# Attention outputs copied out of PSUM before they are scaled, and another plan for the expert blocks, in a top-k attention and mixture-of-experts kernel

## The chip, the cores and the metric

The kernel runs on one core of one Trainium2 chip. A core has five engines with queues of their own, each in order: TensorE (PE in the rows; PEld is its weight load, which overlaps it), VectorE (DVE), ScalarE (ACT), GpSimd (POOL) and SyncE (SP), which here only issues transfers. They wait for each other through semaphores. The metric is the device time of one execution in microseconds; lower is better. Before the change it is 1802.71 us, the median of three runs (1800.99 to 1813.61 us).

## The reference

Eight batches, eight heads, 576 positions of 64 numbers each, all float32. Each query keeps the keys whose score is among its 32 largest. The result, 4608 rows of 512 numbers, goes through a layer of eight experts: each row takes the one expert with the largest logit.

```python
scores = scale * np.matmul(q, k.transpose(0, 1, 3, 2))
kth = np.partition(scores, -32, axis=-1)[..., -32:-32 + 1]
scores = np.where(scores >= kth, scores, -1000000000.0)
attn = softmax(scores)                      # sum + 1e-09 below the line
x = np.matmul(attn, v)                      # to (4608, 512): row, head*64
logits = x @ w_gate                         # (4608, 8)
expert_idx = np.argmax(logits, axis=1)
gate_w = softmax(logits)[row, expert_idx]   # sum + 1e-09 below the line
y[row] = np.maximum(x[row] @ w1[expert], 0) @ w2[expert]   # 512 -> 1024 -> 512
return gate_w[:, None] * y
```

## The kernel before

**Two kinds of work.** The first is attention, in 8 batches of 4 *units*; a unit is a pair of heads of one batch, so there are 32. A unit is worked in 5 *items* (`groups`): four items of two tiles of 128 queries, one for each head, and a fifth of the 64 left-over queries of both. The second is the experts' work, in *blocks* of 128 rows that belong to one expert. A block reads its rows (`xg`), 2 MB of w1 and 2 MB of w2, and writes its rows out.

**One item** goes round the engines: TensorE multiplies q by k into PSUM (`scores`, L213), ScalarE copies the scores to SBUF (`s`, L218), VectorE folds them in two halves (`hl`, L225 and L226) and finds the 32nd largest with MAX8 and MATCH_REPLACE8 (L248 to L269, `thr`), GpSimd makes a bound of it (`low`, L271), ScalarE and GpSimd make the masked scores (`w`, L283 and L293), ScalarE takes the exponential (L296) and sums a row into `z`, TensorE transposes `w` (L309, L317) and ScalarE copies that out (L312, L320). Scores are issued two items ahead of the search.

**One unit** ends in `outputs` (L324): `po` = weights times v (L339), copied to `oT` (L340), transposed back into the PSUM tile `px` (L343) and `pl` (L345), and multiplied by the gate's weights into `pl` (L348). The closure `scaled` that it returns runs later, in `settle`, after the search of the next unit's second item: VectorE takes 1/z (`rz`, L356 to L358), multiplies `px` and `pl` by it on the way into the SBUF rows `x` (L361, L365), does the same for the logits (`lt`, L369) and adds them to `lg` (L373 to L376). `px` and `pl` lie in PSUM until then.

**One batch** ends, in the `settle` of its fourth unit, in `route` (L379): argmax, rank of each row inside its expert, place in the scratch array `x_rows`; five scatters on GpSimd (L420) write the rows there. Then `table` (L442) lists the blocks that are now full: `sure[b]` is the number that must be full after batch b whatever the routing, 0, 2, 6, 11, 15, 20, 24 after batches 0 to 6. After the last batch the table has 19 slots, which with the 24 are the 43 (`NSLOT`) that any routing needs at most; slots without rows read an empty block and are computed like the rest.

**What sets the order.** The loop over 160 items (L605 on) calls `search`, `settle`, `close` (transposes and, at a unit's end, `outputs`), `depths`, `scores` of the item after next, `weights`, and then `pieces`, which issues some of the 17 pieces of a block: its transposes (L506), w1 (L516, rows named `ph`), w2 (L525, `py`). Pieces are issued only from the sixth item of a batch on (`FIRST` = 5), the number being what is left divided by the items left in the batch, so that a batch's blocks are done by its end; in the last batch two blocks (`KEEP`) are held back to cover the last batch's route. A scheduler then sets each engine's order from these calls: it may move an instruction past others of its engine where data allow. Two blocks are loaded ahead (`ahead`, L566), on SP's queue, where the loads of q, k and v stand too (L186, L189); a block's load waits until its rows are scattered. After the last batch `fill_up` writes empty rows behind each expert's last one, and the last table's blocks follow one after another. At the end every engine loads the flag `any_i` (L644) and branches past an exact second version, which does not run.

## Time and profile before

| what | value |
|---|---|
| median of three runs | 1802.71 us (1800.99 to 1813.61) |
| the profiled execution | 1800.4 us; its span, from the first to the last instruction, 1798.7 us |
| busy share of the span | PE 83%, PEld 54%, DVE 71%, ACT 51%, POOL 35% |
| transfers | 244.06 MB, mean 136 GB/s |
| TensorE's granted clock, mean | 0.87 |

The busy shares are means over stages that differ: until about 1453 us attention runs, with blocks between from the third batch on; after that only blocks do, and DVE is idle. So the rows below are read stage by stage. A row of a stretch gives its start and end, its length, then for PE, PEld, DVE, ACT and POOL the busy time in it with the number of instructions, then the granted clock of TensorE (1.00 is 2.4 GHz, 0.50 is 1.2 GHz), the share of the DMA engines and GB/s. A unit is counted from one multiplication of `px` on VectorE (L361) to the next, so the first four of those behind 64.0 us are units 1 to 4. In a row, "busy" is the time in which the engine executes, an idle time is that just before an instruction, and the name behind "<-" is what ended it.

### The profile page before, as it was taken

How to read it: one execution, taken by the hardware profiler on the slowest of the kernel's cores; microseconds unless marked ns; L12 is line 12 of the kernel's file. 1: busy time of each engine (PE TensorE's matmuls, PEld its weight loads, DVE VectorE, ACT ScalarE, POOL GpSimd, SP SyncE). 2: the span in 40 equal slices, each digit the busy share in tenths (PEclk: the TensorE clock that was granted, in tenths of full speed). 3: DMA queues.
4: the chain of work that ended last, by engine and by line, in shares of the span. 5: the costliest groups of instructions: out<-in, count | busy, mean ns of one | idle time of the engine just before them, and what ended most of it. 6: DMA issues, size and time to landing. Idle time of an engine off the chain costs nothing. (4 is left out here: it accounts for less than half of the span.)

```text
span 1798.7 us, 25580 instructions
## 1 busy us (share of the span) xinstructions
PE 1499.2 (83%) x8126; PEld 963.9 (54%) x8126; DVE 1280.0 (71%) x4391; ACT 914.2 (51%) x1845; POOL 624.7 (35%) x876
## 2 busy tenths in 40 slices
PE   5777687679778996999879996999789958999996
PEld 3444444345445663565546654666455536666664
DVE  8999899999999889977788888967799910000000
ACT  5665566657656665655546665655466711111111
POOL 3444444344444434433344344433344420000000
PEclk8667777769967999999959997999788988999999
DMA  1000100061015331644062406433163238888883
GB/s 54 22 21 21 47 28 27 29 233 40 27 47 220 118 141 54 225 167 171 33 238 97 156 34 227 145 131 128 39 234 113 106 101 311 297 303 299 299 297 144
DMA packets 107567, 244.06 MB, mean 136 GB/s; under 512 B 5534, under 2 KB 26014, under 8 KB 107424
## 3 DMA queue, kind: packets, MB, share of 16 engines
q1 hardware_dynamic: 101040, 223.43, 34.7%
q0 software_dynamic: 6384, 18.92, 2.9%
q8 instruction: 66, 1.08, 0.2%
q14 instruction: 77, 0.63, 0.1%
HBM read 221.05 MB, written 23.11 MB: 136 GB/s over the span
## 5 line engine op out<-in xcount | busy, mean ns | idle before, releaser
L293 POOL TENSOR_TENSOR w<-s,w 128x576 f32<-128x576 f32 x288 | 432.2, 1517 | 280.6 <-ACT w L283 278.7
L516 PE MATMUL ph<-xTs,w 128*128 128x128 f32 x2752 | 348.4, 284 | 24.7 <-ACT xTs L508 19.9
L309 PE MATMUL wTm<-ident,w 128*128 128x128 f32 x1152 | 211.0, 325 | 181.0 <-ACT w L296 176.6
L516 PEld LDWEIGHTS ph<-xTs,w 128*128 128x128 f32 x2752 | 328.9, 198 | 53.2 <-ACT xTs L508 27.9
L248 DVE MAX8 tops<-scr 128x8 f32<-128x288 f32 x864 | 355.3, 445 | 1.2
L213 PE MATMUL sc<-qkb 64*128 64x288 f32 (+1 forms) x1280 | 339.9, 522 | 17.5 <-ACT s L218 10.7
L525 PE MATMUL py<-w,hT 128*128 128x512 f32 x688 | 319.5, 610 | 0.0
L296 ACT ACTIVATE w<-w,nbias 128x576 f32<-128x576 f32 x288 | 223.3, 776 | 184.0 <-POOL w L293 182.8
L309 PEld LDWEIGHTS wTm<-ident,w 128*128 128x128 f32 x1152 | 155.3, 165 | 258.0 <-ACT w L296 227.4
L283 ACT ACTIVATE w<-s,low 128x576 f32<-128x576 f32 x288 | 212.7, 774 | 119.9 <-POOL low L271 119.6
L256 DVE MATCH_REPLACE8 scr<-tops,scr 128x288 f32<-128x288 f32 x576 | 250.3, 440 | 0.1
L213 PEld LDWEIGHTS sc<-qkb 64*128 64x128 f32 (+1 forms) x1280 | 164.7, 213 | 112.2 <-issue 41.9
L218 ACT COPY s<-sc 128x576 f32<-128x576 f32 x288 | 175.1, 637 | 59.8 <-PE sc L213 44.2
L525 PEld LDWEIGHTS py<-w,hT 128*128 128x128 f32 x688 | 127.5, 195 | 145.5 <-issue 145.5
L312 ACT COPY wT<-wTm 128x512 f32<-128x512 f32 x256 | 143.9, 586 | 72.0 <-PE wTm L309 71.1
L225 DVE TENSOR_TENSOR hl<-s 128x576 f32<-128x576 f32 (+1 forms) x160 | 131.9, 824 | 56.9 <-ACT s L218 56.0
L530 POOL DMA_INDIRECT out_dram<-y,xg x43 | 43.5, 1012 | 336.0 <-ACT y L529 331.0
L339 PE MATMUL po<-wT,vb 128*64 128x288 f32 x1024 | 151.0, 441 | 8.7 <-ACT wT L314 8.7
L250 POOL TENSOR_SCALAR nbias<-tops 128x2 f32<-128x2 f32 (+1 forms) x160 | 34.9, 218 | 303.9 <-DVE thr L269 178.4
L521 ACT ACTIVATE hT<-ph 128x512 f32<-128x512 f32 x86 | 51.0, 593 | 173.8 <-PE ph L516 173.4
L226 DVE TENSOR_TENSOR hl<-s 128x576 f32<-128x576 f32 (+1 forms) x160 | 127.1, 794 | 0.0
L256 DVE MATCH_REPLACE8 scr<-tops,hl 128x288 f32<-128x288 f32 x288 | 125.4, 440 | 0.0
(115 smaller groups left out, 1283.5 us busy)
## 6 DMA issues: line engine op xcount, KB each, us to landing
w<-in_moe_w_dram SPq DMA_DIRECT2D x86, 2048.0 KB, 12.9
qkb<-in_qk_dram SPq DMA_DIRECT2D x32, 576.0 KB, 3.8
xg<-x_rows SPq DMA_DIRECT2D x43, 257.0 KB, 2.8
vb<-in_v_dram SPq DMA_DIRECT2D x32, 320.0 KB, 3.1
x_rows<-blank SPq DMA_DIRECT2D x9, 257.0 KB, 6.7
out_dram<-y,xg POOLq DMA_INDIRECT x43
x_rows<-x,posi POOLq DMA_INDIRECT x40
wg<-in_moe_w_gate_dram SPq DMA_DIRECT2D x1, 16.0 KB
```

The costliest lines, as they stand in the source:

```text
L213: nc.tensor.matmul(ps[rows, j, 0:HF], n.q[d, cols], n.k[d, j * HF:(j + 1) * HF], start=True, stop=True)
L218: nc.scalar.copy(s[:, m, :, :], ps[:, :, 0:HF])
L248: nc.vector.max(out=tops[:, m, r * 8:(r + 1) * 8], in_=src[m])
L256: nc.vector.match_replace(out=scr[:, m, :], in_to_replace=tops[:, m, r * 8:(r + 1) * 8], in_values=src[m], imm_value=NEG,)
L283: nc.scalar.activation(w[:, m, :], s[:, m, :, :].rearrange("p j k -> p (j k)"), AF.Relu, scale=-STEEP, bias=low[:, m:m + 1],)
L293: nc.gpsimd.tensor_tensor(w[:, m, :], s[:, m, :, :].rearrange("p j k -> p (j k)"), w[:, m, :], op=ALU.subtract)
L296: nc.scalar.activation(w[:, m, :], w[:, m, :], AF.Exp, scale=scale, bias=nbias[:, m:m + 1], accum_out=n.z[:, c + m:c + m + 1],)
L309: nc.tensor.transpose(pm[:, c * P:(c + 1) * P], w[:, m, c * P:(c + 1) * P], ident)
L312: nc.scalar.copy(n.wT[:, :, m, tiles[0] * P:(tiles[0] + 1) * P], pm4)
L339: nc.tensor.matmul(po[r, 0:HF], lhsT, rhs, start=(c == 0), stop=(c == KC - 1))
L516: nc.tensor.matmul(ph[:, f, :], n.w1[:, 0, dt, fc * P:(fc + 1) * P], xT[:, dt, :], start=(dt == 0), stop=(dt == DT - 1),)
L525: nc.tensor.matmul(py, hT[:, f, :], n.w2[:, 0, f, :], start=(f == 0), stop=(f == FT - 1))
```

## The change

`outputs` copies `px`, `pl` and the logits out of PSUM at once on ScalarE, into `x` and `lt`. `scaled` is now a function of its own: 1/z stays on VectorE, and the multiplications by it and the additions to `lg` run on GpSimd, in SBUF. `route` gives back its five scatters as closures, which the loop calls one per item (all at once after the last batch). The blocks listed after batches 0 to 6 are no longer those that must be full but those that usually are (`upto_of`): 0, 4, 8, 13, 17, 22, 26; a slot that is not filled becomes the empty block. They are released (`waiting`, `ahead`) when the batch's scatters have been called, and their pieces are issued at an even `rate` over 20 items, from the sixth item of one batch to the fifth of the next. In the last batch the number is again what is left by the items left. `pinned` ties each of a block's TensorE instructions behind the last attention instruction of TensorE issued before it (`last_pe`, an order without a wait). After the last batch 14 blocks (`ALWAYS`) always run, and the 5 slots that are left of 19 (`spare`) stand behind a branch on the count `rest_i`.

```diff
-    sure = [max(0, -((E * (P - 1) - S * (b + 1)) // P)) for b in range(B - 1)] + [NSLOT]
+    sure = [max(0, -((E * (P - 1) - S * (b + 1)) // P)) for b in range(B - 1)]
+    upto_of = [max(0, (S * (b + 1) - E * ST) // P - 1) for b in range(B - 1)]
+    upto_of = [max(a, c) if b else 0 for b, (a, c) in enumerate(zip(sure, upto_of))]
+    new_of = [b - a for a, b in zip([0] + upto_of, upto_of)]
...
+    LAST = NSLOT - sure[-1]
+    ALWAYS = EB + E // 2 - upto_of[-1]
...
+        nc.scalar.copy(x[:, 0:NC, n.u * P:(n.u + 1) * P], px[:, :].rearrange("p (t d) -> p t d", t=NC))
         pl = bank("pl")
...
+        nc.scalar.copy(x[:, NC, n.u * P:(n.u + 1) * P], pl[:, 0:P])
+        n.lt = k.small.tile([P, KC, 2, E], F32, name="lt")
+        nc.scalar.copy(n.lt, pl[:, P:P + KC * lw].rearrange("p (t h e) -> p t h e", t=KC, h=2))
+
+    def scaled(n, x, lg):
+
+        rz = rz_of[n.u % 2]
+        if not k.exact:
+            nc.vector.tensor_tensor(doubt, doubt, n.over, op=ALU.max)
+        nc.vector.tensor_scalar_add(rz[:, 0:NT], n.z, EPS)
+        nc.vector.reciprocal(rz[:, 0:NT], rz[:, 0:NT])
+        nc.vector.tensor_copy(rz[0:ST, NT:NT + 1], rz[ST:P, NT - 1:NT])
+        rzb = rz[:, :].rearrange("p (t h) -> p t h", h=2)
+        nc.gpsimd.tensor_tensor(n.lt, n.lt, _inner(rzb, E), op=ALU.mult)
+        if n.u:
+            nc.gpsimd.tensor_tensor(lg, lg, n.lt[:, :, 0, :], op=ALU.add)
+            nc.gpsimd.tensor_tensor(lg, lg, n.lt[:, :, 1, :], op=ALU.add)
+        else:
+            nc.gpsimd.tensor_tensor(lg, n.lt[:, :, 0, :], n.lt[:, :, 1, :], op=ALU.add)
+        xu = x[:, :, n.u * P:(n.u + 1) * P].rearrange("p t (h d) -> p t h d", h=2)
+        nc.gpsimd.tensor_tensor(xu, xu, _inner(rzb, D), op=ALU.mult)
...
+    def pinned(put):
+
+        if k.last_pe is not None and not k.exact:
+            tc.add_manual_dep(put.ins, k.last_pe.name, AFTER)
+        return put
+
...
+        def scatter(n):
+            nonlocal left
+            for _ in range(min(n, len(scatters))):
+                scatters.pop(0)()
+            if not scatters and coming:
+                waiting.extend(coming)
+                left += len(coming) * PIECES
+                coming.clear()
                 ahead()
...
+            scatter(1)
             at = i % per_batch
-            if at >= FIRST:
-                rest = left - (KEEP if b == B - 1 else 0)
-                pieces(-(-rest // (per_batch - at)))
+            if at == FIRST and b:
+                rate = new_of[b - 1] * PIECES / per_batch
+            credit += rate
+            room = left - (KEEP if b == B - 1 else 0)
+            if b == B - 1 and at > FIRST:
+                credit = room / (per_batch - at)
+            n_now = min(int(credit + 1e-6), room)
+            credit -= n_now
+            pieces(n_now)
         close(last)
         settle()
-        pieces(left)
+        kept = left - ALWAYS * PIECES
+        assert kept == KEEP
+        pieces(kept)
+        k.last_pe = None
+        pieces(ALWAYS * PIECES)
+        for _ in current:
+            pass
+        more = nc.values_load(rest_i[0:1, 0:1], min_val=0, max_val=LAST)
+        with tc.If(more > ALWAYS):
+            for slot in spare:
+                for _ in block(load_block(*slot)):
+                    pass
```

What this does to the engines' order is shown at three places. The first is VectorE in the `settle` of an ordinary unit in the sixth batch; `rz` is 1/z, `px` and `pl` the PSUM tiles, `hl` the fold of an item. Before:

```order
L356 TENSOR_SCALAR rz_102<-z 128x9
L265 TENSOR_TENSOR both<-tops_94 128x18
L357 RECIPROCAL rz_102<-rz_102 128x9
L269 TENSOR_REDUCE thr<-both 128x2
L358 COPY rz_102<-rz_102 64x1
L361 TENSOR_TENSOR x<-px,rz_102 128x4x128
L365 TENSOR_TENSOR x<-pl,rz_102 128x128
L225 TENSOR_TENSOR hl<-s 128x576
L226 TENSOR_TENSOR hl<-s 128x576
L369 TENSOR_TENSOR lt<-pl,rz_102 128x80
L248 MAX tops_88<-hl 128x8
L373 TENSOR_TENSOR lg<-lg,lt 128x40
```

With the change (its line numbers are higher by some ten):

```order
L373 TENSOR_SCALAR rz_102<-z 128x9
L277 TENSOR_TENSOR both<-tops_94 128x18
L374 RECIPROCAL rz_102<-rz_102 128x9
L281 TENSOR_REDUCE thr<-both 128x2
L375 COPY rz_102<-rz_102 64x1
L237 TENSOR_TENSOR hl<-s 128x576
L238 TENSOR_TENSOR hl<-s 128x576
L260 MAX tops_88<-hl 128x8 x2
L265 MAX tops_88<-hl 128x8 x2
L268 MATCH_REPLACE scr<-tops_88,hl 128x288 x2
```

Between 1/z and the next fold no instruction that reads `px` or `pl` is left, and the logits' instructions are gone from VectorE.

The second is TensorE in the last batch, from the end of its first unit on; `sc` are scores, `wTm` and `wTl` transposed weights, `ph` and `py` a block's two products, `xtp` its transposes. Before:

```order
L348 MATMUL pl<-wg_72,oT_96 128x16 x5
L213 MATMUL sc<-qkb 128x288
L516 MATMUL ph<-xTs,w_11835 128x128 x12
L213 MATMUL sc<-qkb 64x288
L309 MATMUL wTm<-ident,w 128x128 x8
L213 MATMUL sc<-qkb 64x288 x3
L516 MATMUL ph<-xTs,w_11835 128x128 x2
L317 MATMUL wTl<-ident,w 64x128 x2
L516 MATMUL ph<-xTs,w_11835 128x128
L309 MATMUL wTm<-ident,w 128x128 x4
L516 MATMUL ph<-xTs,w_11835 128x128 x3
L309 MATMUL wTm<-ident,w 128x128 x4
```

With the change:

```order
L522 MATMUL xtp<-ident,xg 128x128 x4
L321 MATMUL wTm<-ident,w 128x128 x7
L532 MATMUL ph<-xTs,w_11288 128x128 x32
L541 MATMUL py<-w_11290,hT 128x512 x8
L522 MATMUL xtp<-ident,xg 128x128 x4
L321 MATMUL wTm<-ident,w 128x128
L329 MATMUL wTl<-ident,w 64x128 x2
L225 MATMUL sc<-qkb 128x288
L532 MATMUL ph<-xTs,w_12319 128x128 x32
L541 MATMUL py<-w_12321,hT 128x512 x8
L522 MATMUL xtp<-ident,xg 128x128 x4
L225 MATMUL sc<-qkb 128x288 x2
```

Where a block's pieces stood between transposes and scores, three whole blocks (32 `ph` and 8 `py` each; the third's `py` follow the last row) now stand one behind another with three of the four score products of one item between them. In batches 3 to 7 the pieces stay spread: each unit's rows hold the pieces of one block, or of one and a quarter where the list has five.

The third is GpSimd around the scatters of the third batch; `x_rows` is the scratch array. Before:

```order
L271 TENSOR_SCALAR low<-thr 128x2
L274 TENSOR_TENSOR over<-tops_90,thr 128x2
L293 TENSOR_TENSOR w<-s,w 128x576 x2
L250 TENSOR_SCALAR nbias<-tops_92 128x2
L420 DMA x_rows<-x,posi 38016x514 x5
L271 TENSOR_SCALAR low<-thr 128x2
L274 TENSOR_TENSOR over<-tops_92,thr 128x2
L250 TENSOR_SCALAR nbias<-tops_94 128x2
```

With the change:

```order
L283 TENSOR_SCALAR low<-thr 128x2
L286 TENSOR_TENSOR over<-tops_90,thr 128x2
L384 TENSOR_TENSOR x<-x,rz_102 128x5x128
L377 TENSOR_TENSOR lt<-lt,rz_102 128x80
L379 TENSOR_TENSOR lg<-lg,lt 128x40
L380 TENSOR_TENSOR lg<-lg,lt 128x40
L305 TENSOR_TENSOR w<-s,w 128x576 x2
L262 TENSOR_SCALAR nbias<-tops_92 128x2
L427 DMA x_rows<-x,posi 38016x514 x5
L283 TENSOR_SCALAR low<-thr 128x2
L286 TENSOR_TENSOR over<-tops_92,thr 128x2
```

The multiplication and the logits' instructions are new, and the five scatters still stand together, as they do in every batch from the third on; only in the first two are they apart.

## Rows read from the trace of the kernel before

**Rows 1.** The page: busy us, share of the span and instructions by engine.

```profile
PE 1499.2 (83%) x8126; PEld 963.9 (54%) x8126; DVE 1280.0 (71%) x4391; ACT 914.2 (51%) x1845; POOL 624.7 (35%) x876
```

**Rows 2.** Busy by stretch: batches, end; us, PE PEld DVE ACT POOL, clock, DMA.

```profile
64.00:397.30 333.30, 239.65 (x1144) 138.50 (x1142) 319.11 (x1078) 204.04 (x418) 145.99 (x202) 0.72 0.16 56
397.30:567.10 169.80, 139.08 (x739) 86.83 (x738) 160.95 (x550) 104.87 (x215) 74.02 (x104) 0.82 0.24 85
567.10:744.40 177.30, 152.97 (x917) 97.89 (x916) 159.12 (x550) 111.20 (x228) 74.87 (x106) 0.96 0.38 137
744.40:944.60 200.20, 175.78 (x943) 114.48 (x944) 158.10 (x550) 110.51 (x222) 78.08 (x106) 0.86 0.39 142
944.60:1128.10 183.50, 160.03 (x916) 101.50 (x918) 160.19 (x550) 112.04 (x228) 76.01 (x107) 0.92 0.37 130
1128.10:1333.80 205.70, 181.16 (x996) 115.30 (x992) 159.24 (x550) 114.99 (x234) 80.54 (x107) 0.88 0.39 139
1333.80:1453.40 119.60, 109.93 (x643) 70.47 (x641) 100.46 (x332) 75.62 (x156) 47.66 (x69) 0.94 0.26 93
1453.40:1798.70 345.30, 297.48 (x1684) 214.76 (x1682) 7.45 (x44) 46.99 (x80) 24.37 (x25) 0.96 0.73 266
```

**Rows 3.** The same of single units: without blocks, with route, with blocks.

```profile
103.50:144.10 40.60, 28.68 (x144) 16.47 (x142) 39.62 (x129) 25.41 (x54) 17.60 (x24) 0.71 0.08 23
184.60:231.00 46.40, 32.59 (x146) 19.20 (x144) 41.29 (x148) 25.70 (x54) 20.65 (x30) 0.71 0.12 41
993.20:1036.70 43.50, 42.11 (x245) 26.25 (x244) 38.15 (x129) 27.79 (x58) 16.69 (x26) 1.00 0.40 136
```

**Rows 4.** Groups by line: busy us, mean ns, idle before and its releaser.

```profile
L312 ACT COPY wT<-wTm 128x512 f32<-128x512 f32 x256 | 143.9, 586 | 72.0 <-PE wTm L309 71.1
...
L361 DVE TENSOR_TENSOR x<-px,rz 128x512 f32<-128x512 f32 x32 | 22.1, 692 | 79.7 <-PE px L343 79.6
...
L374 DVE TENSOR_TENSOR lg<-lg,lt 128x40 f32<-128x40 f32 x24 | 11.5, 481 | 0.2
...
L373 DVE TENSOR_TENSOR lg<-lg,lt 128x40 f32<-128x40 f32 x24 | 10.1, 420 | 0.2
L365 DVE TENSOR_TENSOR x<-pl,rz 128x128 f32<-128x128 f32 x32 | 9.2, 289 | 11.5 <-PE pl L348 11.5
...
L322 ACT COPY wTt<-wTl 64x128 f32<-64x128 f32 x32 | 8.3, 259 | 0.0
L369 DVE TENSOR_TENSOR lt<-pl,rz 128x80 f32<-128x80 f32 x32 | 7.4, 230 | 0.0
```

**Rows 5.** One line each: ns min/median/max, first and last start.

```profile
L374 DVE TENSOR_TENSOR lg<-lg,lt x24: 176/199/1075, 106.6 to 1455.3; 128x40 f32<-128x40 f32 x24
...
L225 DVE TENSOR_TENSOR hl<-s x160: 434/749/1930, 9.4 to 1432.1; 128x576 f32<-128x576 f32 x128, 128x288 f32<-128x288 f32 x32
...
L293 POOL TENSOR_TENSOR w<-s,w x288: 1392/1410/2717, 20.4 to 1441.6; 128x576 f32<-128x576 f32 x144
```

**Rows 6.** The order of time, TensorE, one block of the last stage: start, us.

```profile
1506.28 0.60 PE L506 MATMUL xtp<-ident,xg 128*128 128x128 f32 x4
...
1507.74 7.41 PE L516 MATMUL ph<-xTs,w 128*128 128x128 f32 x64 [0.86 <-ACT xTs L508]
...
1514.99 7.03 PE L525 MATMUL py<-w,hT 128*128 128x512 f32 x16
...
1521.86 0.60 PE L506 MATMUL xtp<-ident,xg 128*128 128x128 f32 x4
```

**Rows 7.** The page, transfers: KB each, median us from issue to landing.

```profile
w<-in_moe_w_dram SPq DMA_DIRECT2D x86, 2048.0 KB, 12.9
```

**Rows 8.** The branch at the end, in the queues: ns min/median/max, starts.

```profile
L644 POOLq TENSOR_LOAD <-any_i x1: 496/496/496, 1787.8 to 1787.8; - x1
...
L645 PEldq COMPARE_BRANCH  x1: 3355/3355/3355, 1781.4 to 1781.4; - x1
...
L645 POOLq INC_SWDGE_SEM x1: 1859/1859/1859, 1789.1 to 1789.1; - x1
```

More of the change, by code (lines that the diff above doesn't have):

```diff
@@ L14 @@
 AX = mybir.AxisListType
+AFTER = mybir.DependencyInfo(mybir.DependencyClass.NoSync, mybir.DependencyReason.DATA)
 WAIT = mybir.DependencyInfo(mybir.DependencyClass.Sync, mybir.DependencyReason.DATA)
@@ L152 @@
     nc.vector.tensor_copy(run, e_at)
+    rest_i = const.tile([1, 1], I32, name="rest_i")
     done = const.tile([1, E], F32, name="done")
@@ L322, in transposed, with outputs @@
             nc.scalar.copy(n.wTt[:, :, SM:S], pt[0:ST, 0:P].rearrange("p (h q) -> p h q", h=2))
-    def outputs(n):
-        rz = rz_of[k.unit % 2]
+    def outputs(n, x):
         oT = oT_of[k.unit % 2]
@@ L417, in route, with scatter @@
         mine = []
-        for i in range(KC):
+        def scatter(i):
             r = slice(0, P if i < NC else ST)
@@ L427, in route @@
                 mine.append(put)
-        scattered.extend(mine)
+                scattered.append(put)
+        return [lambda i=i: scatter(i) for i in range(KC)]
     def fill_up():
@@ L472, in table @@
         )
[L473 to L477 removed]
+        none = sm.tile([1, NSLOT], F32, name="none")
+        nc.vector.tensor_scalar(none[:, 0:n], slots[:, 0:n], upto[:, E - 1:E], float(EMPTY), ALU.is_ge, ALU.mult)
+        nc.vector.tensor_tensor(slot_f[:, 1, 0:n], slot_f[:, 1, 0:n], none[:, 0:n], op=ALU.max)
+        nc.vector.tensor_scalar_min(slot_f[:, 1, 0:n], slot_f[:, 1, 0:n], float(EMPTY))
         slot_i = sm.tile([1, 2, NSLOT], I32, name="slot_i")
         nc.vector.tensor_copy(slot_i[:, :, 0:n], slot_f[:, :, 0:n])
[L480 removed]
+        if last:
+            nc.vector.tensor_copy(rest_i, upto[:, E - 1:E])
+        else:
             nc.vector.tensor_tensor(upto, left, upto, op=ALU.subtract)
@@ L546 @@
         x_of, lg_of = {}, {}
-        waiting = []
-        loaded = []
+        waiting, loaded, coming, spare, scatters = [], [], [], [], []
         current = None
@@ L574, in close @@
             if g == groups[-1]:
-                late = (b, u, outputs(n))
+                if u == 0:
+                    x_of[b] = k.xp.tile([P, KC, XW], F32, name="x")
+                    token_ids(x_of[b][:, :, Dm + 1].bitcast(I32), b)
+                    lg_of[b] = k.small.tile([P, KC, E], F32, name="lg")
+                outputs(n, x_of[b])
+                late = (b, u)
                 b2, u2 = divmod(b * U + u + 2, U)
@@ L583, in settle @@
                 return
-            b, u, scaled = late
+            b, u = late
             late = None
-            if u == 0:
-                x_of[b] = k.xp.tile([P, KC, XW], F32, name="x")
-                token_ids(x_of[b][:, :, Dm + 1].bitcast(I32), b)
-                lg_of[b] = k.small.tile([P, KC, E], F32, name="lg")
-            scaled(x_of[b], lg_of[b])
+            scaled(unit_of[b, u], x_of[b], lg_of[b])
             if u < U - 1:
                 return
-            route(x_of[b], lg_of[b])
+            scatters.extend(route(x_of[b], lg_of[b]))
             if b == B - 1:
+                scatter(KC)
                 fill_up()
-            new = sure[b] - (sure[b - 1] if b else 0)
+            new = LAST if b == B - 1 else new_of[b]
             if new:
                 slot_i = table(new, b == B - 1)
-                waiting.extend((slot_i[0:1, 0, j:j + 1], slot_i[0:1, 1, j:j + 1]) for j in range(new))
-                left += new * PIECES
+                coming.extend((slot_i[0:1, 0, j:j + 1], slot_i[0:1, 1, j:j + 1]) for j in range(new))
+                if b == B - 1:
+                    spare.extend(coming[ALWAYS:])
+                    del coming[ALWAYS:]
+            if b == B - 1:
+                scatter(0)
+        def scatter(n):
[6 more added lines that the diff above has]
+                coming.clear()
                 ahead()
@@ L611 @@
         last = None
+        credit = rate = 0.0
         for i, (b, u, g) in enumerate(work):
@@ L666 @@
                         transposed(n, g, w)
-                    outputs(n)(x, lg)
-                route(x, lg)
+                    outputs(n, x)
+                    scaled(n, x, lg)
+                for put in route(x, lg):
+                    put()
                 nc.vector.tensor_scalar_add(ids, ids, S)
```

51 lines of the change are left out of this document (11 added, 40 removed).

## The prediction

> **What bounds the kernel now.** The busy shares of the page name no engine: TensorE has 83% of the span, VectorE 71% [rows 1]. The busy times by stretch do. Up to 397 us there are no blocks: a unit takes 40.60 us and VectorE is busy for 39.62 of them [rows 3], so VectorE bounds it. From the third batch on there are blocks, and a batch takes 169.8, 177.3, 200.2, 183.5 and 205.7 us while VectorE stays at 158 to 161 [rows 2]: it waits there for 9 to 46 us a batch. In a unit of that stage TensorE is busy for 42.11 of 43.50 us at the full granted clock [rows 3]. After 1453 us there are only blocks, each 15.6 us after the one before: 0.60 + 7.41 + 7.03 us of TensorE and 0.86 us of waiting for ScalarE [rows 6].
>
> The groups by line say what VectorE waits for: its multiplication of `px` stood idle for 79.7 us in 32 units and that of `pl` for 11.5 us, both until TensorE was done [rows 4]. So whenever TensorE has blocks in front of a unit's last products, VectorE, which is in order, stops there, and the search of the next items is late too.
>
> **The change, part by part.**
>
> *Scaling on GpSimd.* Five kinds of instruction leave VectorE: 22.1 + 9.2 + 7.4 + 10.1 + 11.5 us [rows 4], with those of a batch's first unit 62.5 us, or 1.95 us a unit. With them go the two waits. The copies cost ScalarE 0.59 us for `px` (the copy of 128x512) and about 0.26 us each for `pl` and `lt` (that of 64x128 has the same 128 elements a partition) [rows 4]: 1.1 us a unit on an engine that is busy for 27.8 of 43.5 us [rows 3], so nothing. If that cover were gone it would be 1.1 us a unit, 35 us in all. On GpSimd the multiplication of `x` has 640 elements a partition where the nearest row, `w`, has 576 and takes 1.41 us, 2.72 at most [rows 5]: 1.6 us, at most 3.0. With the logits I take 2.3 us a unit, and GpSimd is busy for 17 of 41 us [rows 3]: hidden as well.
>
> What isn't hidden is that the two engines get into each other's way. An addition to `lg` on VectorE takes 199 ns at the median and 1075 at most, a fold 749 and 1930 [rows 5]: the long ones are those that meet a multiplication on GpSimd. A fold that is met loses up to 1.2 us. Bounds for the new work: no fold met, 0; two a unit, 2.4 us. I take 0.6, one fold in two units, since the new multiplication begins after the copies and so mostly behind the two folds that follow 1/z. So a unit bound by VectorE loses 1.95 us of work and 0.9 us of waiting and gets 0.6 back: 2.2 us less.
>
> The Trainium skill speaks against this part (SBUF — State Buffer, "Who interferes with whom"): GpSimd and a VectorE instruction with two SBUF inputs take one shared read interface, and the later one is blocked for the whole of the earlier. The long rows of L374 and L225 agree with it.
>
> *A unit with route.* It takes 46.40 us without blocks [rows 3]. VectorE's first step of `route` needs `lg`, which now comes by ScalarE (1.1 us) and GpSimd (2.3 us), where VectorE itself took 2 us. So only about 1 us is won in such a unit. The scatters are five in a row again from the third batch on (the order above), so spreading them gives nothing there.
>
> *Blocks over 20 items instead of 15.* TensorE's work for attention in a unit: the unit with 42.11 us held 36 `ph`, 13 `py` and 4 transposes of blocks, which by [rows 6] are 36/32 x 7.41 + 13/8 x 7.03 + 0.60 = 20.4 us; 21.7 us are left. With one block a unit (lists of four) TensorE needs 21.7 + 15.0 = 36.7 us, VectorE 38.15 - 1.95 + 0.6 = 36.8. With one and a quarter (lists of five) TensorE needs 21.7 + 18.8 = 40.5 us. A unit can't be shorter than that; where one engine clearly bounds it, it was 1.4 us longer [rows 3]. Two engines that are even cost each other more: I take 41 us for the first (between 37 and the row's 43.5) and 43.5 for the second (between 40.5 and, with the 6 us that separate 37 from 43.5, 46.5). Units with route: 45.5 and 47, and 45 in the seventh batch's, which holds few pieces.
>
> *The pieces of the last batch.* The number to issue is computed with `room` = left - KEEP, which is negative while fewer than 34 pieces are left, in the first five items. Then `n_now` is negative and `credit` grows, so that the sixth item issues all it has at once. The order shows it: three blocks in a row in the second unit. They take 3 x 15.6 = 47 us of TensorE. Of the next items only one is scored ahead and not yet searched, 8 us of VectorE (40.60 / 5, [rows 3]). So VectorE stands still for 39 us, and nothing makes it up. This stretch was 119.6 us with 100.46 us of VectorE [rows 2]; now it is 100.5 - 3 x 1.95 + the same 19 us of idle time + 39 = 153 us.
>
> *Fewer blocks.* By the reference's own inputs the experts get 620, 519, 615, 513, 642, 507, 554 and 638 rows, which is 40 blocks; in the lists after batches 0 to 6 no slot stays empty, and 14 are left for the end: the branch isn't taken. Where 24 + 19 blocks ran, 26 + 14 do. The end has 16 blocks (2 kept) instead of 21. The two kept ones now run whole behind the last unit, 31 us, and the gap that they cover is longer (from 1453.4 us to 15.6 us before 1506.3, 37 us [rows 2, 6]): hidden. So 5 x 15.6 = 78 us go.
>
> *The branch.* Each engine loads a register and jumps; on GpSimd, which ends last, 0.50 + 1.86 us [rows 8]; TensorE's compare stood for 3.36 us, though under its own matmuls. Bounds 2.4 and 5.8; I take 3. The last unit's scaling goes by ScalarE and GpSimd, 2 us later than before: the gap is that much longer.
>
> The Trainium skill (Runtime: NRT & Kernel Launch, "Instruction fetch mechanics") says that a taken branch to a target outside the fetched window has to wait for a fetch; no row here shows one by itself. The bounds above don't use it.
>
> *The sum*, against the profiled execution [rows 2]: before 64.0 us nothing. To 397.3 us: 6 x 2.2 + 2 x 1 = 15 less. The five batches with blocks: 169.8 to 168.5, 177.3 to 168.5, 200.2 to 177.5, 183.5 to 168.5, 205.7 to 175.5: 78 less. The last batch: 33 more. The end: 78 less, 2 + 3 more. 1798.7 - 15 - 78 + 33 - 73 = 1665.7 us, with the 1.7 us that lie around the span 1667.4. The median of the three runs is 2.3 us above the profiled one, which is no more than their spread; I say 1668 us.
>
> **Rivals.**
>
> *GpSimd takes over VectorE's wait.* Its `lt` and `x` wait for the same `px` and stand in order before the next `w`; if that holds the scores' buffers, units with blocks stay as they were. For it: GpSimd waits in the same place in its order. Against it: VectorE still has two scored items in hand, 16 us. Then the 78 us are not won: 1746 us.
>
> *The lock.* If two folds a unit are met (2.4 us), the 20 units that VectorE bounds or nearly so (8 + 9 + 3) lose 1.8 us more: 1704 us; with GpSimd's multiplication at 3.0 us and the other units hit too, 1668 + 31 x 1.8 = 1724 us. The rule of the Trainium skill named above (SBUF — State Buffer, "Who interferes with whom") would make it this one.
>
> *The units come down to their floor*, 37 and 40.5 us: 9 x 4 + 6 x 3 = 54 us less, 1614; half of that, 1641 us, is likelier.
>
> *The change doesn't skip what it says.* If more than 14 blocks were left, the five spare ones run: 78 us more, and a pipeline that starts anew, some 15: 1761 us. The row counts speak against it.
>
> *Slower than before: the weights.* Pinned pieces stand in TensorE's order in front of attention; if a block's weights come late, everything stops. A load takes 12.9 us [rows 7]; uncovered in all 24 blocks, 310 us: 1978 us. From 134 / 24 = 5.6 us a block it is slower than before. Against it: SP issues a block's load when the block two before is done, and a block now lasts 33 to 41 us.
>
> **The numbers.** The forecast as worked out, 0.64; GpSimd takes over the wait 0.10; the lock 0.12; the floor 0.09; spare blocks run 0.01; weights late 0.04, of which half is slower than before and half within a percent of it. The low end, 1628, is halfway into the floor; the high end, 1725, is the lock at its worst; outside lie the rivals beyond and the rest of the floor, about 0.2. A measurement of this kernel can tell about 1%, 18 us: faster 0.96, the same 0.02, slower 0.02.
>
> **What would show it.** Right: VectorE's idle time in front of a read of `px` gone, with no like wait in front of its folds; units of 41 us where a list has four, 43 to 44 where it has five; in the last batch one hole of about 39 us in VectorE while TensorE does 96 `ph` and 24 `py`; 16 blocks at 15.6 us behind the last unit; the branch under 6 us. Wrong: folds that wait for `s` as long as they waited for `px`; folds at 1.9 us at the median; long waits of `ph` for a transfer; the hole absent; or a block cadence other than 15.6 us.

## The result

The median is 1705.33 us (four runs, 1699.89 to 1713.96) against 1802.59 us for the kernel before: a ratio of 0.945 (0.940 to 0.951). The change makes the kernel 97 us faster; 135 were forecast. The profiled execution took 1705.1 us, its span 1703.2.

The busy time by stretch, with borders that answer to those of [rows 2]: a stretch runs from the transposed `px` of a batch's first unit to that of the next batch's first unit, the last batch's to that of its last unit (columns as there, with the number of instructions in brackets):

```profile
63.80:398.60 334.80, 256.31 (x1137) 145.89 (x1135) 308.07 (x1054) 210.87 (x444) 163.59 (x234) 0.68 0.15 50
398.60:572.80 174.20, 159.88 (x901) 100.64 (x899) 153.31 (x516) 115.98 (x237) 84.53 (x118) 0.94 0.38 134
572.80:745.60 172.80, 161.99 (x903) 101.74 (x901) 156.14 (x534) 115.52 (x237) 85.37 (x121) 0.94 0.39 139
745.60:922.70 177.10, 163.90 (x972) 103.22 (x972) 153.92 (x539) 114.64 (x239) 83.40 (x124) 1.00 0.46 158
922.70:1100.50 177.80, 164.68 (x918) 103.95 (x916) 156.53 (x528) 117.09 (x240) 87.22 (x119) 0.94 0.39 138
1100.50:1277.80 177.30, 155.07 (x888) 97.08 (x888) 157.32 (x543) 112.50 (x235) 79.96 (x119) 0.93 0.35 123
1277.80:1434.30 156.50, 126.86 (x654) 78.44 (x652) 98.10 (x316) 80.96 (x167) 53.95 (x81) 0.79 0.36 129
1434.30:1703.20 268.90, 238.86 (x1361) 172.71 (x1359) 5.96 (x40) 39.13 (x68) 22.60 (x25) 0.97 0.72 258
```

Beside the forecast:

| stretch | before | forecast | after | after less forecast |
|---|---|---|---|---|
| to the second batch's end | 333.3 | 318.3 | 334.8 | +16.5 |
| third batch | 169.8 | 168.5 | 174.2 | +5.7 |
| fourth | 177.3 | 168.5 | 172.8 | +4.3 |
| fifth | 200.2 | 177.5 | 177.1 | -0.4 |
| sixth | 183.5 | 168.5 | 177.8 | +9.3 |
| seventh | 205.7 | 175.5 | 177.3 | +1.8 |
| last batch | 119.6 | 153 | 156.5 | +3.5 |
| the end | 345.3 | 272.3 | 268.9 | -3.4 |

At the ends of the batches the borders of [rows 2] lie where VectorE begins to wait for `px`, 0.5 to 4.9 us before its multiplication starts. By the starts of the multiplications the stretches before are 333.9, 170.2, 176.8, 204.6, 181.7, 203.3, 118.9 and 345.3 us; the sum of the forecast is the same by both.

So four of the eight stretches are within 4 us, and the miss of 37 us sits where a unit has no block or one block. A unit without blocks was 40.60 us and is 40.60 us, though VectorE is busy 2 us less in it than in [rows 3]; one with route is not shorter either:

```profile
127.50:168.10 40.60, 32.46 (x141) 17.96 (x141) 37.60 (x124) 26.31 (x56) 18.79 (x28) 0.67 0.08 23
168.10:214.60 46.50, 32.11 (x144) 18.77 (x144) 42.30 (x143) 26.42 (x56) 24.16 (x34) 0.72 0.13 46
```

In the unit without blocks VectorE stands idle for 3.0 us now, where it was 1.0 us in [rows 3]. What it waits for (us in total, times, longest us), before, beside the 79.6 us in front of its read of `px` [rows 4], and now:

```profile
DVE hl L225 <- ACT s L218: 56.0, 32, 5.5
```

```profile
DVE hl L237 <- ACT s L230: 150.3, 51, 40.9
DVE mx L388 <- POOL lg L380: 23.4, 8, 13.4
```

The wait for `px` is gone, and the fold of the copied scores waits instead: 150.3 us, of which 40.9 are the hole in the last batch. Of the 23.4 us in front of `mx`, the first step of `route`, 13.4 lie behind the last unit, 3.8 and 4.1 in the first two batches, and at most 0.5 in each of the others.

**Where ScalarE stands.** The same place in a unit without blocks, ScalarE in order of time (start, us; in brackets the idle time before and what ended it). Before:

```profile
102.91 1.18 ACT L218 COPY s<-sc 128x576 f32<-128x576 f32 x2
103.97 1.46 ACT L283 ACTIVATE w<-s,low 128x576 f32<-128x576 f32 x2
106.28 0.78 ACT L296 ACTIVATE w<-w,nbias 128x576 f32<-128x576 f32 x1 [0.86 <-POOL w L293]
...
107.54 1.07 ACT L312 COPY wT<-wTm 128x512 f32<-128x512 f32 x2 [0.39 <-PE wTm L309]
```

After:

```profile
103.62 1.18 ACT L230 COPY s<-sc 128x576 f32<-128x576 f32 x2
104.69 0.61 ACT L355 COPY x<-px 128x512 f32<-128x512 f32 x1
...
106.92 1.07 ACT L324 COPY wT<-wTm 128x512 f32<-128x512 f32 x2 [1.30 <-PE wTm L321]
107.88 0.79 ACT L295 ACTIVATE w<-s,low 128x576 f32<-128x576 f32 x1
...
111.10 0.78 ACT L308 ACTIVATE w<-w,nbias 128x576 f32<-128x576 f32 x1 [1.05 <-POOL w L305]
```

And two rows of VectorE after, the end of that item's search and the fold that then stands:

```profile
102.86 0.15 DVE L281 TENSOR_REDUCE thr<-both 128x2 f32<-128x18 f32 x1
```

```profile
122.10 0.76 DVE L237 TENSOR_TENSOR hl<-s 128x576 f32<-128x576 f32 x1 [2.94 <-ACT s L230]
```

The search ends at 103.0 us, and the depths (`w<-s,low`), the next step of that item, start 4.9 us later. Ahead of them in ScalarE's order stand the three new copies (one row of three is shown) and two copies of transposed weights, for which ScalarE waits 1.30 us more. Before, the depths started at 103.97 us, and the copies of transposed weights stood behind them. So the order changed by more than the three copies: in the 31 units behind the first, the second item's depths stood ahead of the first item's copies of transposed weights in all 31 before, and do so in 11 now. The exponential, which follows by way of GpSimd, comes at 111.10 where it came at 106.28; the copies of the scores of a later item stand behind that; and the fold waits 2.94 us for them.

### The profile page after: what moved, and what is told of

The parts are those of the page before. It is cut to its first block, busy times and chain, and to the rows that moved or that the text cites. A ratio compares the mean times of both kernels' runs of the same rounds, so it can differ in the third digit from the quotient of the medians.

```text
span 1703.2 us, 24993 instructions
## 1 busy us (share of the span) xinstructions
PE 1470.7 (86%) x7874; PEld 927.9 (54%) x7874; DVE 1245.2 (73%) x4258; ACT 940.7 (55%) x1929; POOL 683.8 (40%) x993
## 5 line engine op out<-in xcount | busy, mean ns | idle before, releaser
L305 POOL TENSOR_TENSOR w<-s,w 128x576 f32<-128x576 f32 x288 | 427.9, 1498 | 263.9 <-ACT w L295 263.3
L225 PE MATMUL sc<-qkb 64*128 64x288 f32 (+1 forms) x1280 | 358.7, 514 | 7.7 <-DMA qkb<-in_qk_dram 5.6
L321 PE MATMUL wTm<-ident,w 128*128 128x128 f32 x1152 | 219.5, 330 | 158.0 <-ACT w L308 157.0
L532 PE MATMUL ph<-xTs,w 128*128 128x128 f32 x2560 | 325.9, 286 | 16.3 <-ACT xTs L524 12.9
L532 PEld LDWEIGHTS ph<-xTs,w 128*128 128x128 f32 x2560 | 308.2, 199 | 44.6 <-issue 20.9
L321 PEld LDWEIGHTS wTm<-ident,w 128*128 128x128 f32 x1152 | 156.5, 167 | 256.5 <-ACT w L308 235.3
L541 PE MATMUL py<-w,hT 128*128 128x512 f32 x640 | 294.6, 601 | 0.0
L237 DVE TENSOR_TENSOR hl<-s 128x576 f32<-128x576 f32 (+1 forms) x160 | 141.3, 883 | 150.6 <-ACT s L230 150.3
L541 PEld LDWEIGHTS py<-w,hT 128*128 128x128 f32 x640 | 115.5, 191 | 122.5 <-issue 122.2
L238 DVE TENSOR_TENSOR hl<-s 128x576 f32<-128x576 f32 (+1 forms) x160 | 131.7, 823 | 0.0
L260 DVE MAX8 tops<-hl 128x8 f32<-128x288 f32 x288 | 125.4, 441 | 0.0
```

Source lines behind the costliest of these rows:

```text
L225: k.last_pe = nc.tensor.matmul(ps[rows, j, 0:HF], n.q[d, cols], n.k[d, j * HF:(j + 1) * HF], start=True, stop=True).ins
L260: nc.vector.max(out=tops[:, m, r * 8:(r + 1) * 8], in_=src[m])
L305: nc.gpsimd.tensor_tensor(w[:, m, :], s[:, m, :, :].rearrange("p j k -> p (j k)"), w[:, m, :], op=ALU.subtract)
L321: nc.tensor.transpose(pm[:, c * P:(c + 1) * P], w[:, m, c * P:(c + 1) * P], ident)
L532: pinned(nc.tensor.matmul(ph[:, f, :], n.w1[:, 0, dt, fc * P:(fc + 1) * P], xT[:, dt, :], start=(dt == 0), stop=(dt == DT - 1),))
L541: pinned(nc.tensor.matmul(py, hT[:, f, :], n.w2[:, 0, f, :], start=(f == 0), stop=(f == FT - 1)))
```

## The experiments

Each ratio is against the kernel before, in the same set of runs. Medians of the kernel before in these sets: 1804.85, 1804.70 and 1802.37 us.

**The scaling back on VectorE, the rest of the change kept.**

```diff
-        nc.scalar.copy(x[:, 0:NC, n.u * P:(n.u + 1) * P], px[:, :].rearrange("p (t d) -> p t d", t=NC))
...
-        nc.gpsimd.tensor_tensor(xu, xu, _inner(rzb, D), op=ALU.mult)
+        nc.vector.tensor_tensor(xu[:, 0:NC], px[:, :].rearrange("p (t h d) -> p t h d", t=NC, h=2),
+            _inner(rzb[:, 0:NC, :], D), op=ALU.mult)
```

> The changed kernel with the scaling as it was before: VectorE multiplies px and pl out of PSUM in settle; the block plan, the pins and the branch stay. Theory Q (the scaling's move won nothing, since ScalarE's three copies and GpSimd's multiplications stand in front of an item's w and the next s and made the fold wait instead): units without blocks stay at 40.5 us, the whole within 15 us of 1705, 1695 to 1720. Rival U (the move took VectorE out of TensorE's queue and made the units with blocks short): the wait for px is back, 60 to 90 us in all, and the whole is 1735 to 1765 us. Rival L (the two engines meet at SBUF): folds fall from 883 to 824 ns at the mean, 14 us, and the whole is about 1690.

Measured: 1699.0 us, 0.942 (0.938 to 0.946). The intervals of this kernel and of the whole change overlap: the change without its first part is as fast as with it. That is theory Q. The units with blocks stay short although VectorE waits for `px` again; the fifth batch takes 178.0 us, where the whole change has 177.1 and the kernel before 204.6:

```profile
DVE hl L237 <- ACT s L230: 81.4, 24, 41.8
DVE x L376 <- PE px L354: 38.3, 19, 8.9
```

```profile
738.70:916.70 178.00, 165.99 (x960) 104.31 (x959) 158.27 (x551) 112.67 (x227) 74.93 (x109) 0.98 0.44 154
```

So it isn't the freed `px` that shortened the batches with blocks. And in a unit without blocks (41.0 us) no fold waits.

**The kernel before with the scaling moved, and nothing else.** The edit is the first part of the diff alone (copies on ScalarE, products on GpSimd).

> The kernel before with the scaling's move alone: copies on ScalarE, multiplications on GpSimd; the block plan is that of before. Q: 1790 to 1815 us, the same as before, with VectorE's wait for px (91 us) gone and its wait for s up from 56 by 80 to 110 us. U: 1740 to 1770. L: slower by some 14 us, 1815, with longer folds.

Measured: 1805.45 us, 1.001 (0.998 to 1.003): no change. Its waits:

```profile
DVE hl L225 <- ACT s L218: 153.2, 51, 8.6
DVE mx L376 <- POOL lg L368: 35.4, 8, 12.6
```

The 79.6 + 11.5 us in front of `px` and `pl` are gone, the folds' wait has grown from 56.0 to 153.2 us, and `mx` adds 35.4. So 133 us of waiting came for 91 that went, and the difference is about what VectorE's busy time fell by (from 1280.0 to 1241.2 us). The fifth batch stays long:

```profile
757.60:959.80 202.20, 180.29 (x983) 116.65 (x982) 155.53 (x548) 116.77 (x240) 87.67 (x122) 0.87 0.40 142
```

**The pieces of the last batch issued evenly.**

```diff
-            n_now = min(int(credit + 1e-6), room)
-            credit -= n_now
+            n_now = max(0, min(int(credit + 1e-6), room))
+            credit = min(credit - n_now, 1.0)
```

> The changed kernel with the number of pieces kept from going negative and the credit capped at one: the last batch's three blocks are spread over its last 15 items. If the three blocks in a row cost what the prediction says (a hole of about 39 us in VectorE, 33 us more than before in the last batch): 1665 to 1675 us, and the hole is gone. If the blocks only move the same wait to later units: 1690 to 1705.

Measured: 1677.15 us, 0.930 (0.926 to 0.933), 28 us less than with the bunch. The end of the changed kernel's bunch: the last of its three blocks on TensorE with the scores behind it, and then the fold on VectorE that waited for them:

```profile
1312.54 7.41 PE L532 MATMUL ph<-xTs,w 128*128 128x128 f32 x64 [0.18 <-ACT xTs L524]
1319.79 7.03 PE L541 MATMUL py<-w,hT 128*128 128x512 f32 x16
1326.75 0.75 PE L225 MATMUL sc<-qkb 64*128 64x288 f32 x2
```

```profile
1328.20 0.76 DVE L237 TENSOR_TENSOR hl<-s 128x576 f32<-128x576 f32 x1 [40.88 <-ACT s L230]
```

With even pieces the longest wait in front of a fold is 5.8 us, and the last batch takes 117.4 us instead of 156.5. TensorE's granted clock in that batch is 0.99 where it was 0.79: with the bunch no block was left behind it to stand between the attention's products, and from 1370 us on the clock was 0.64. So the 28 us are the hole and this together.

**GpSimd's multiplication of x made small.** It scales one column in 64 only, so most of `x` stays unscaled; the instruction stays in its place.

```diff
-        nc.gpsimd.tensor_tensor(xu, xu, _inner(rzb, D), op=ALU.mult)
+        nc.gpsimd.tensor_tensor(xu[:, :, :, 0:1], xu[:, :, :, 0:1], _inner(rzb, 1), op=ALU.mult)
```

> The changed kernel with GpSimd's multiplication of x by 1/z cut to one of 64 columns (the rest of x is left unscaled; the routing doesn't use it): an instruction of 640 elements becomes one of 10, and some 1.1 us a unit leave GpSimd. If GpSimd's part of Q is the loop's cost: 25 to 35 us less, 1670 to 1680. If ScalarE's copies are: 1698 to 1707. L: folds shorter, 14 us less, 1690.

Measured: 1713.49 us, 0.950 (0.945 to 0.954), not faster than the whole change (0.940 to 0.951). The multiplication fell from 1259 to 231 ns, and the folds' wait stayed:

```profile
L384 POOL TENSOR_TENSOR x<-x,rz 128x10 f32<-128x10 f32 x32 | 7.4, 231 | 28.0 <-ACT x L364 28.0
...
L237 DVE TENSOR_TENSOR hl<-s 128x576 f32<-128x576 f32 (+1 forms) x160 | 133.3, 833 | 146.9 <-ACT s L230 146.7
```

Neither the time of that multiplication nor its meeting VectorE is what holds the units. GpSimd still stands for 28.0 us in front of it until ScalarE's copies are done; this run leaves that as it was.

**The depths first on ScalarE.** The changed kernel; `depths` is called before `settle` and `close`, and the copies of transposed weights are ordered behind it.

```diff
+            w = depths(g, s_of[i], low)
             settle()
             if last is not None:
                 close(last)
-            w = depths(g, s_of[i], low)
...
+    def behind(copy):
+        if k.last_act is not None and not k.exact:
+            tc.add_manual_dep(copy.ins, k.last_act.name, AFTER)
```

> The changed kernel with one thing moved: an item's depths (the Relu on ScalarE that follows the search) are put ahead of the previous unit's copies out of px and pl, and the copies of the transposed weights are held behind them. Theory S (it is the place of the new copies in ScalarE's order that eats what VectorE saves: in a unit without blocks the depths start 3.9 us later than before, the scores' copy with them, and the fold stands for 2.9 us): a unit without blocks takes 37.5 to 39 us where it took 40.4, and the whole 1665 to 1690 us. Theory G (the work on GpSimd, or the engines' shared reading, holds the unit, whatever ScalarE's order): 40 to 41 us a unit and 1698 to 1712 us. Held copies can also cost: if the transposed weights come late for the outputs, units with blocks get longer and the whole is above 1712.

Measured: 1639.35 us, 0.909 (0.906 to 0.912): 66 us less than the whole change, below the range of theory S. A unit without blocks takes 36.3 us, all of it VectorE's:

```profile
85.20:121.50 36.30, 27.42 (x142) 15.56 (x142) 36.24 (x124) 26.02 (x55) 18.67 (x28) 0.78 0.08 26
```

ScalarE in order of time, where the search had ended at 99.1 us:

```profile
99.54 0.78 ACT L296 ACTIVATE w<-s,low 128x576 f32<-128x576 f32 x1 [1.45 <-POOL low L284]
...
101.55 0.59 ACT L361 COPY x<-px 128x512 f32<-128x512 f32 x1 [0.28 <-PE px L360]
...
102.96 0.79 ACT L309 ACTIVATE w<-w,nbias 128x576 f32<-128x576 f32 x1
```

The depths now wait for `low`, which is to say that ScalarE is there before its input is; the copies run while GpSimd makes `w`. The copies are as long as they were. Only their place differs. GpSimd stands in front of its multiplication of `x` for 24.1 us here too (29.1 in the changed kernel), so that wait isn't what held the units either.

Of the 4.3 us between 40.60 and 36.30, VectorE's idle time makes 2.9 (from 3.0 to 0.1) and its busy time 1.4 (from 37.60 to 36.24).

**The depths first, the copies of transposed weights not held.** The first half of that edit alone.

> The changed kernel with the depths issued before the previous unit's copies, but without holding the copies of the transposed weights behind them: those go where they went, ahead of the depths in many items. Theory S1 (the three copies out of px and pl, 1.1 us, are what delays the depths): as with all held, 1639 us, at most 1650. Theory S2 (it is the copies of transposed weights and TensorE's transposes that they wait for, and the new copies only came on top): the units without blocks stay at 39.5 to 40.5 us, the whole 1680 to 1705 us.

Measured: 1715.58 us, 0.950 (0.945 to 0.954), not separable from the change by itself, and outside the ranges of both theories. A unit without blocks, and ScalarE at the place shown above:

```profile
126.50:166.00 39.50, 31.73 (x141) 17.95 (x142) 36.48 (x124) 26.17 (x56) 18.91 (x29) 0.67 0.08 24
```

```profile
104.59 0.61 ACT L355 COPY x<-px 128x512 f32<-128x512 f32 x1
...
107.64 1.45 ACT L295 ACTIVATE w<-s,low 128x576 f32<-128x576 f32 x2
```

The depths still stand behind the three new copies, 5.7 us after the search ended (101.9 us). The second item's depths are ahead of the copy of `px` in 7 of the 31 units behind the first; in the changed kernel it is 6, and in the run before this one all 31. So the earlier call alone doesn't put the depths first, since the scheduler orders ScalarE anew; only with the hold do they come first. VectorE's idle time in the unit is 3.0 us, as with the change by itself, and the 1.1 us that it is shorter are one instruction's: the maximum into `doubt`, 128x9 elements, takes 0.14 us here and 1.25 us there, where it meets a multiplication of GpSimd.

So this run doesn't tell S1 from S2. Without the three copies (the run with the scaling back) no fold waits in such a unit, so they bring the wait; whether by their own 1.1 us or by the copies of transposed weights that come to stand in front as well was not told apart. The granted clock doesn't decide it: this unit has 0.67 and the one before it 0.72, and both take 39.50 us.

**The kernel before with the depths first.** Both halves of the edit, without any of the change.

> The kernel before with the depths first and the copies of the transposed weights held behind them, all else as it was. Theory C (before the change ScalarE's order cost little, since VectorE was busy for 39.62 of 40.60 us in a unit without blocks, and stood for px where there are blocks): at most 1 us a unit without blocks, the whole 1785 to 1808 us. Rival D (the order held the units with blocks before the change too, the waits for px being a consequence of it): 1720 to 1775 us.

Measured: 1767.02 us, 0.981 (0.977 to 0.986): 35 us less, outside theory C's range and inside rival D's. The order on ScalarE cost the kernel before as well. VectorE's idle time in front of `px` is down from 79.6 to 63.8 us:

```profile
DVE x L368 <- PE px L350: 63.8, 17, 9.2
```

and in a unit without blocks VectorE's busy time, with the same instructions as in [rows 3], from 39.62 to 37.6 us:

```profile
86.50:126.90 40.40, 29.95 (x142) 16.60 (x142) 37.62 (x129) 25.53 (x52) 16.50 (x24) 0.71 0.08 23
```

**Fewer blocks at the end, in the kernel before.**

```diff
-                waiting.extend((slot_i[0:1, 0, j:j + 1], slot_i[0:1, 1, j:j + 1]) for j in range(new))
+                run_new = new if b < B - 1 else new - 3
+                waiting.extend((slot_i[0:1, 0, j:j + 1], slot_i[0:1, 1, j:j + 1]) for j in range(run_new))
```

> The kernel before, with the last list's three slots that are empty at the end not run, so that 24 + 16 blocks run instead of 24 + 19. Nothing else is changed. Theory B (a block behind the last unit is worth its cadence of 15.6 us): 3 x 15.6 = 47 us less, about 1756 us. Rival: the end is also bound by the loads of weights or the stores, and a block fewer is worth less, 1765 to 1790 us.

Measured: 1757.28 us, 0.972 (0.968 to 0.977): 47 us for three blocks (42 to 58 by the interval), 15.8 each.

**Even pieces without the pins**, the run with even pieces where `pinned` ties nothing.

> The changed kernel with even pieces in the last batch and without the pins that hold a piece in its place in TensorE's order. Theory P0 (the order on TensorE is the same with and without pins, but for the last batch and the first list): within 6 us of the run with even pieces alone, 1671 to 1683 us. Rival P1 (pins win by holding a block's pieces apart): 1690 us or more. Rival P2 (pins lose, since TensorE stands in order behind a piece): 1665 us or less.

Measured: 1677.09 us, 0.928 (0.925 to 0.931), the same as with the pins. They neither win nor lose here.

**Three combinations.** Even pieces with the scaling back on VectorE:

> The changed kernel with two parts changed: the scaling stands on VectorE again, straight out of PSUM, and the last batch's pieces are issued evenly (the number to issue is never negative and credit is not saved up). If the two act apart, as the run with the scaling back (6 us less) and the run with even pieces (28 us less) have them: 1671 us. If the even pieces need the freed px (VectorE waits again for px in the last batch): 1680 to 1700 us. If GpSimd's copies were the cost of the route units in the last batch as well: 1660 to 1668 us.

Measured: 1654.36 us, 0.917 (0.914 to 0.919). That is 23 us less than even pieces alone, and less than each of the three expectations: without the depths first, the move of the scaling costs time once the bunch is gone. The two edits did not act apart. In the profiled executions the difference lies in the third and the sixth batch above all: 165.5 and 170.2 us here, 177.7 and 179.8 with even pieces alone.

Depths first and even pieces:

> The changed kernel with the depths first, as in the run of that, and with even pieces in the last batch. If the two act apart (1639 for the first, 28 us less for the second): 1611 us. If VectorE, which waits less for the scores with the depths first, loses as much to the bunch as with the scaling back (46 us): 1593 us. If TensorE bounds the last batch anyway: 1625 us or more.

Measured: 1602.15 us, 0.888 (0.885 to 0.891), the fastest of all: 103 us below the change as it stands and 200 below the kernel before. Even pieces give 37 us here, between the 28 and the 46 of the expectation.

The same with the scaling back on VectorE:

> The changed kernel with depths first, even pieces, and the scaling back on VectorE out of PSUM. Theory M (with ScalarE's order mended, the move of the scaling to GpSimd is worth what VectorE saves, some 2 us in a unit bound by VectorE): units without blocks 38 to 39.5 us, 15 to 40 us more than depths first with even pieces. Rival N (the move is worth nothing in any order, since GpSimd and ScalarE give it back in units with route and blocks): within 10 us of it, and below 1620 us.

Measured: 1605.55 us, 0.891 (0.887 to 0.894), not separable from the run before it, as rival N has it for the whole. But they get there by different ways. The units without blocks are longer with the scaling on VectorE, as theory M has it:

```profile
88.10:128.50 40.40, 29.94 (x142) 16.56 (x144) 37.60 (x131) 25.52 (x52) 16.53 (x24) 0.71 0.08 23
128.50:166.70 38.20, 28.10 (x142) 15.79 (x144) 37.59 (x130) 25.35 (x52) 16.51 (x24) 0.77 0.08 25
```

VectorE is busy for 37.6 us in both, 1.0 us more than in such a unit with the scaling on GpSimd (36.64 of 36.70 us). The 2.2 us between the two rows are TensorE's: in the first, 16 products of `po` take 4.11 us at a granted clock of 0.50, in the second 2.16 us at 1.00, and VectorE waits 2.3 us for `px` in the first alone. To the second batch's end the run with the scaling on VectorE takes 322.1 us and the other 308.1. It wins 5.0 of these 14 us back in the six batches that follow, and 4.5 at the end (267.0 against 271.5 us).

## Why the prediction came out as it did

**Right: the fewer blocks.** Five blocks at 15.6 us were the largest safe term. The end took 268.9 us where 272.3 were forecast, the cadence is that of [rows 6], and the run with three blocks fewer gave 47 us by itself:

```profile
1501.58 0.60 PE L522 MATMUL xtp<-ident,xg 128*128 128x128 f32 x4
...
1517.16 0.60 PE L522 MATMUL xtp<-ident,xg 128*128 128x128 f32 x4
```

**Right: the branch.** The last `py` ended 11.8 us before the end of the span before the change (1786.9 of 1798.7) and ends 14.3 us before it now: 2.5 us, 3 forecast. The last `py`, before and after:

```profile
1779.90 7.03 PE L525 MATMUL py<-w,hT 128*128 128x512 f32 x16
```

```profile
1681.85 7.03 PE L541 MATMUL py<-w,hT 128*128 128x512 f32 x16
```

**Right: the bunch in the last batch.** Forecast a hole of 39 us and a last batch 33 us longer; measured a hole of 40.88 us and 36.9 us longer, and 28 us of the whole when it is undone.

**Right in size, wrong in reason: batches with longer lists.** The fifth and seventh came out at 177.1 and 177.3 us (177.5 and 175.5 forecast). The prediction gave VectorE's freedom from `px` as part of the reason. But with the scaling back on VectorE the batches are as short (178.0 and 182.5 us), and with the scaling moved alone they stay long (202.2 and 199.0), so as far as that reason goes the size came out by luck. The pins are ruled out by the run without them. What is left of the change there is that the 17 pieces of a block are spread over 20 items instead of 15, and, in the seventh batch, that one block less lies in it (62 rows of `py` against 80, 16 to a block). This is concluded from what is left; the spreading was not run by itself.

**Wrong: the stretch without blocks (16.5 of the 37 us, of which 6 x 2.2 = 13 were the units without route).** The step that failed is "1.1 us a unit on an engine that is busy for 27.8 of 43.5 us [rows 3], so nothing". VectorE's part of the sum held: 1.95 - 0.6 = 1.35 us less of busy time was forecast, and it went from 39.62 to 37.60, 2.0 less. But its idle time went from 1.0 to 3.0 us, 2.9 of them in front of one fold, where the sum had it fall by 0.9. ScalarE's busy share was taken for cover. ScalarE is in order and stands in the loop by which one item's search leads to the scores of a later one (search, `low`, depths, `w`, exponential, copy of the scores, fold). Its idle time is spent waiting inside that loop, so a copy ahead of the depths pushes the loop, whatever the share. The run with the depths first shows it: same copies, same GpSimd work, 36.3 us a unit, of which VectorE is idle for 0.1. The prediction had priced the lost cover at "1.1 us a unit, 35 us in all"; that this is near the miss of 37 us is luck, since such a unit loses 2.9 us and the batches with longer lists lose nothing.

**Wrong by the same step: units with route and lists of four (19.3 of the 37 us, in the third, fourth and sixth batches).** The miss lies in the three units with route: they take 51.1, 52.2 and 52.1 us where 45.5 was forecast, 18.9 of the 19.3 us; the nine units between them take 41.0 on the mean, and 41 was forecast. The unit with route of the fourth batch with the change, with the scaling back on VectorE, and with the depths first:

```profile
693.40:745.60 52.20, 45.70 (x246) 30.54 (x244) 43.84 (x162) 30.36 (x63) 26.49 (x35) 0.87 0.46 164
```

```profile
690.70:738.70 48.00, 42.19 (x246) 27.30 (x244) 45.62 (x178) 28.30 (x57) 22.59 (x32) 0.93 0.54 192
```

```profile
657.60:703.60 46.00, 40.99 (x236) 25.39 (x234) 42.96 (x164) 30.16 (x62) 24.39 (x36) 0.93 0.56 198
```

The prediction looked at `lg`, which comes later ("only about 1 us is won in such a unit"). That wait cost 0.5 us here, and some 4 us only in the first two batches. Of the 8.4 us for which VectorE is idle in the first row, 5.3 lie in front of folds. With the depths first the three units take 142.0 us instead of 155.4: that is 13.4 of the 18.9 us by ScalarE's order. What the other 5.5 are was not found.

The instructions were sized well: ScalarE's copies are 592 + 267 + 234 ns (1.1 us forecast), GpSimd's part 467 + 423 + 304 ns for the logits and 1259 for `x`, 2.45 us in all (2.3 forecast):

```profile
L384 POOL TENSOR_TENSOR x<-x,rz 128x640 f32<-128x640 f32 x32 | 40.3, 1259 | 29.1 <-ACT x L364 29.1
```

**The rivals.** The first (the wait that takes the place of the one removed) had the right place to look, "folds that wait for `s`", and the wrong engine: ScalarE, not GpSimd. The run with GpSimd's multiplication made small rules that instruction's time out, and the run with the depths first its wait for the copies. The measured 1705 us is the lock's time (1704), by coincidence: that rival asked for 2.4 us a unit in the folds. The lock was priced well: the folds' means went from 824 and 794 ns to 883 and 823, 5 x (59 + 29) ns = 0.44 us a unit where 0.6 was taken. Of it, the run with the small multiplication gives back 883 - 833 = 50 ns in the first half of a fold, and no time. By the Trainium skill (SBUF — State Buffer, "Who interferes with whom") a VectorE instruction with two inputs in SBUF contends with a GpSimd instruction that reads SBUF. The rows agree, and what the new multiplication adds of it didn't decide the time. The third rival's units of 37 us are not far once the depths are first: the third and the fourth batch take 163.4 and 164.5 us then, where 168.5 was forecast. (The low end of the range, 1628 us, was called halfway into that rival; by its own figures half is 1641 and 1628 three quarters.) The fourth rival (spare blocks) and the weights that come late did not show: 40 blocks ran, and TensorE waited for weights in front of `ph` for 2.9 us in all.

## What to carry to other kernels

An engine's idle share is no cover for new work on it when the engine is in order and part of the loop that carries one item to the next: look at what stands behind the new instruction in that engine's order, and put the step that the next item needs first. When a wait is removed, run the removal alone: here it was worth 0, and the wait came back on the next fold. When an instruction is called earlier, look in the trace whether it runs earlier: the scheduler may leave the order as it was. A counter that may go below zero in a schedule's arithmetic is worth as much as a whole mechanism (28 us here).

## What the runs showed of the hardware

VectorE's busy time held some 2 us a unit that was no work. An addition to `lg` of 128x40 elements took 420 and 481 ns on the mean in [rows 4]. In a unit without blocks of the kernel before, GpSimd and then VectorE in order of time:

```profile
104.84 2.77 POOL L293 TENSOR_TENSOR w<-s,w 128x576 f32<-128x576 f32 x2 [1.66 <-ACT w L283]
```

```profile
105.39 0.91 DVE L373 TENSOR_TENSOR lg<-lg,lt 128x40 f32<-128x40 f32 x1
...
106.59 1.07 DVE L374 TENSOR_TENSOR lg<-lg,lt 128x40 f32<-128x40 f32 x1
```

The two multiplications of `w` end at about 106.2 and 107.6 us, and the two additions end at 106.30 and 107.66: each is over within 0.06 us of the GpSimd instruction that it met. The same additions in the kernel before with the depths first, where GpSimd's `w` falls elsewhere:

```profile
106.88 0.18 DVE L380 TENSOR_TENSOR lg<-lg,lt 128x40 f32<-128x40 f32 x1
...
107.35 0.18 DVE L381 TENSOR_TENSOR lg<-lg,lt 128x40 f32<-128x40 f32 x1
```

They take 0.18 us each. In the changed kernel the same shows on the maximum into `doubt`: 0.14 to 0.17 us in 20 units, and 0.64 to 1.36 us in the 12 where it meets a multiplication of `w`, ending within 0.04 us of its end. So an engine that the busy time shows as the bound (39.62 of 40.60 us) may owe part of that time to when another engine's work falls; with the order on ScalarE changed it did the same work in 37.6 us. The prediction took those 39.62 us for work, and could not see that the kernel before had 35 us in it that an order of ScalarE would free.
